# Layer 1 of a fused linear-attention and two-layer kernel: three blocks take turns at 6, 5 and 5 features instead of two blocks at 11 and 5, and fp64 weight tiles land in their own places

## The chip, the cores and the metric

One core of one Trainium2 chip. The metric is device time in microseconds from the first to the last instruction of one launch; lower is better. The kernel before takes 913.98 us, the median of 3 runs (913.88 to 915.51).

## The reference, cut to what matters

```python
B, H, S, D = 4, 8, 768, 48; d_model, d_ff = 384, 2048; n_tokens = B * S = 3072
for t in range(S):                       # linear attention with a decaying state
    state = alpha[:, :, t, :, None] * state + einsum('bhd,bhe->bhde', k[:, :, t], v[:, :, t])
    y[:, :, t] = einsum('bhd,bhde->bhe', q[:, :, t], state)
x = y as (3072, 384)
h = x @ w_in1                            # layer 1: a rational function of h, and |h| in its denominator
P = a0 + a1*h + a2*h**2 + a3*h**3;  Q = 1 + |b0|*|h| + |b1|*h**2
x = (P / (Q + 1e-6)) @ w_out1
h = x @ w_in2                            # layer 2
out = (h * cos(h)) @ w_out2
```

The four weight matrices arrive as fp64, so every weight is turned into fp32 on the chip.

## The kernel before, in words

**Attention.** The 768 steps are cut into 6 chunks of 128 (`C`), and a chunk of one batch is a unit: 24 units (`NU`). The loop at the end of the program runs n from -3 to 24; each pass issues the loads that are due (`load`, L243: `kq` 512 KB, `a` 258 KB, `v` 192 KB a unit), stores of finished outputs (`y_store`, L435), fetches of weights (`w_fetch`, L156), and then `attention(n)` (L457), which spreads the work of five units over the engines. On POOL (GpSimd) a pass has two `affine_select` on the score tiles (L346), a product for q (`scale_q`, L323) and one for k (`scale_k`, L318). On PE (TensorE) a pass has scores (L332), the part of the output from the state (L399) and from the scores (L409), the update (L366) and transposes (L354).

**Weights.** A weight tile is 128 x 384 fp64, 384 KB. `w_fetch` loads it raw; `tick` (L186) turns it into fp32 in three steps: two ACT (ScalarE) copies (L72, L73), then one DVE (VectorE) operation (L77), then a second (L78). `w_hi` (L206) rounds it on ACT (L215), and `w_lo` (L218) puts the rest beside it on POOL (L225). PE multiplies hi and lo parts apart, three passes for a product. Layer 1 has 32 tiles, 16 of `w_in` (one a feature, 128 columns of d_ff) and 16 of `w_out`. `SOME` (L28) says in which passes of attention a tile is fetched: 15 in all. Raw tiles land in a free `x` buffer called `spare`, in two `raw` buffers, and later in the place of `a`. `w_order` sorts the tiles by the slot that needs them. `late` gives the outputs of attention's units 8 to 23 the places of the 16 weight tiles that are needed last, until `y_store` has put them into DRAM in slots 1 to 16 of layer 1.

**Layer 1.** A slot n is one call of `layers(n)` (L1228): the first product of one feature of one block of 512 tokens (`gemm1`, L562, 9 matmuls), the steps of `rational` (L615) for the features of the last four slots, the second product of the feature of slot n - 5 (`gemm2`, L578, 9 matmuls into three accumulators), and at the end one or two steps of `tick`. Six blocks of 16 features make 96 slots. Slot 0 comes with attention's pass 20, so the last passes share the engines with slots 0 to 4. `where(n)` (L524) says which block and feature a slot has: block 0 takes features 0 to 10, block 1 the same, then both take features 11 to 15, and blocks 2 to 5 follow with 16 each. So the weights are needed over 32 slots and not over 16. Because block 1 comes between, block 0's accumulators go out to SBUF at the end of a turn: `acc_out` (L586) copies them on ACT (L593), three copies a turn, and adds them on DVE (L597) to the accumulators of the last turn. `x_load` (L674), `x_hi` (L702) and `x_lo` (L706) bring a block's input and split it, one third a slot, in three slots ahead of its first turn.

In a slot DVE has L628, L631, L632, L633 and L640, and ACT L608, L636, L637, L645 and L646; POOL has L613, L638 and L639. The bank that `gemm1(n)` writes is one of four, and comes free when DVE has done L633 of slot n - 1.

**Layer 2** follows with its own order; its 32 weight tiles are fetched and turned during the rest of layer 1 (`w_fetch(3 * NF ...)` from slot 32 on, one step a slot).

All work is issued in the order of the program on each engine, and every DMA goes through SP's queue.

```python
        if n < 2 * H1:
            return 0, *divmod(n, H1)
        if n < 2 * NF:
            blk, f = divmod(n - 2 * H1, NF - H1)
            return 0, blk, H1 + f
...
        if n < 2 * NF:
            if n > 1:
                tick(2 if n > 4 else 1, 1)
        elif n < N1 - NF:
            if not split:
                tick(1, 1)
```

Of the kernel before, what the change touches and what calls it, by code (L numbers as in the profile page):

```python
# [42 lines left out]
def attn_then_two_moe(ctx, tc, kqT, aT, vP, w1i, w1o, ma, mb, w2i, w2o, out):  # L43
# [109 lines left out]
    def in_spare(i):  # L153
        return i < sum(SOME[:-1]) and i % 6 < 4

    def w_fetch(upto):  # L156
# [9 lines left out]
        if in_spare(i):  # L166
            flat = spare[:, 2 * DM * (i % 6):2 * DM * (i % 6 + 1)]
        elif more and i % 4 < 2:
            if not raw_a:
                raw_a.append(const.tile([128, 3 * HP * (C + 1)], I32, tag="a", name="raw_a"))  # L170
            flat = raw_a[0][:, 2 * DM * (i % 2):2 * DM * (i % 2 + 1)]
        else:
            flat = raw_p.tile([128, 2 * DM], I32, tag="raw", name="raw")
# [379 lines left out]
    def gemm1(n):  # L553
# [3 lines left out]
        x = xt[m, blk]  # L557
        i = 0
        for kk in range(NK):
            ks = slice(kk * 128, (kk + 1) * 128)  # L560
            for w, xx in PASSES:
                nc.tensor.matmul(h, ws[0][f][:, w, ks], x[:, xx, kk, :], start=i == 0, stop=i == 8)  # L562
# [964 lines left out]
```

## Time and profile before

| what | us |
|---|---|
| median of 3 runs | 913.98 (913.88 to 915.51) |
| the profiled execution's own time | 913.8 |
| its span, first to last instruction | 912.1 |
| PE busy | 892.4 (98%) |
| POOL busy | 702.9 (77%) |
| ACT busy | 697.1 (76%) |
| DVE busy | 693.9 (76%) |

The granted TensorE clock is 0.996 of full speed over the span. A view by windows gives the busy time of each engine in each stretch; a timeline gives one row for each instruction (or run of equal ones), with start and duration, and in brackets the idle time of the engine before it and what ended that.

### The profile page before, as it was taken

What the parts mean: (1) busy time and instruction counts of PE and PEld (TensorE: products, weight loads), DVE (VectorE), ACT (ScalarE), POOL (GpSimd) and SP (SyncE); (2) the same over time, 40 slices, a digit from 0 to 9 for tenths busy, and PEclk for the clock granted to TensorE, in tenths of its full rate; (3) what the DMA queues carried; (4) which work ended last, traced back from release to release, by engine and by line L of the source; (5) the groups of instructions that cost most, each with busy time, mean ns of one, the idle gap of its engine ahead of it and who ended that gap; (6) DMA issues with size and microseconds to landing.
All of it is one profiled execution on the core that took longest, in us unless ns stands there. A gap on an engine that the chain in (4) does not pass through costs nothing.

```text
span 912.1 us, 16494 instructions
## 1 busy us (share of the span) xinstructions
PE 892.4 (98%) x5732; PEld 741.2 (81%) x5732; DVE 693.9 (76%) x1247; ACT 697.1 (76%) x1302; POOL 702.9 (77%) x699
## 2 busy tenths in 40 slices
PE   7999999999999999999999999999999999999997
PEld 7788777887788888888888888878888888888885
DVE  7989799998999989989979767666366554555552
ACT  5999898989889788888788778656577666666653
POOL 6899998999889888889879668669787475655332
PEclk9999999999999999999999999999999999999999
DMA  8999545211233141232165276630243433533432
GB/s 281 357 366 370 191 124 196 82 63 36 104 107 94 57 142 45 87 107 94 53 205 185 95 238 239 202 110 27 74 134 109 161 113 96 167 102 105 139 105 90
DMA packets 67307, 128.87 MB, mean 141 GB/s; under 512 B 6928, under 2 KB 30224, under 8 KB 67216
## 3 DMA queue, kind: packets, MB, share of 16 engines
q1 hardware_dynamic: 67216, 127.74, 43.1%
q8 instruction: 47, 0.77, 0.4%
q14 instruction: 44, 0.36, 0.1%
HBM read 95.21 MB, written 32.51 MB: 140 GB/s over the span
## 4 chain that ended last, share of the span: by engine, by line
PE 72%; DVE 8%; ACT 7%; POOL 6%; DMA 4%; issue 2%; SPq 0%; DVEq 0%; ACTq 0%
PE acc L578 22%; PE b L562 18%; PE acc L1054 15%; PE b L1019 6%; PE r L1019 5%; PE r L562 4%; POOL kq L323 2%; POOL kq L318 2%; DMA kq<-kqT 2%; DVE g L628 1%; DVE z L631 1%; ACT b L645 1%; DVE g L640 1%; DMA a<-aT 1%; PE b L1198 1%
## 5 line engine op out<-in xcount | busy, mean ns | idle before, releaser
L578 PE MATMUL acc<-hi,w 128*128 128x512 f32 x738 | 252.5, 396 | 0.0
L562 PE MATMUL b<-x,w 128*128 128x512 f32 x927 | 233.8, 397 | 1.3 <-DVE g L633 1.1
L613 POOL TENSOR_TENSOR lo<-g,hi 128x512 fp32r<-128x512 f32 x128 | 170.2, 1330 | 66.2 <-ACT hi L608 59.4
L562 PEld LDWEIGHTS b<-x,w 128*128 128x128 f32 x927 | 173.4, 188 | 45.4 <-DVE g L633 4.1
L578 PEld LDWEIGHTS acc<-hi,w 128*128 128x128 f32 x738 | 138.7, 188 | 33.9
L1111 POOL TENSOR_TENSOR lo<-g,hi 128x512 fp32r<-128x512 f32 x64 | 83.0, 1297 | 103.6 <-ACT hi L1110 91.6
L578 PE MATMUL acc<-lo,w 128*128 128x512 f32 x369 | 145.7, 395 | 0.0
L639 POOL TENSOR_TENSOR z<-z,ah 128x512 f32<-128x512 f32 x96 | 124.7, 1299 | 8.0
L1054 PE MATMUL acc<-hi,w_out 128*128 128x512 f32 x384 | 130.3, 395 | 0.0
L608 ACT ACTIVATE hi<-g 128x512 fp32r<-128x512 f32 x128 | 80.4, 628 | 47.8 <-PE acc L578 32.6
L578 PEld LDWEIGHTS acc<-lo,w 128*128 128x128 f32 x369 | 69.4, 188 | 16.5
L638 POOL TENSOR_SCALAR z<-ah,cq 128x512 f32<-128x512 f32 x96 | 74.4, 775 | 5.5 <-ACT ah L636 5.4
L1054 PE MATMUL acc<-lo,w_out 128*128 128x512 f32 x192 | 76.4, 398 | 0.4 <-POOL lo L1111 0.2
L1054 PEld LDWEIGHTS acc<-hi,w_out 128*128 128x128 f32 x384 | 68.7, 188 | 9.9
L640 DVE TENSOR_TENSOR g<-g,b 128x512 f32<-128x512 f32 x72 | 49.1, 682 | 16.2 <-ACT g L637 16.0
L636 ACT ACTIVATE ah<-b 128x512 f32<-128x512 f32 x72 | 42.8, 594 | 19.9 <-PE b L562 19.6
L562 PE MATMUL r<-x,w 128*128 128x512 f32 x225 | 56.8, 397 | 1.0 <-DVE g L633 1.0
L1096 DVE SCALAR_TENSOR_TENSOR ah<-z,b 128x512 f32<-128x512 int32 x44 | 30.2, 685 | 35.9 <-ACT z L1092 35.9
L637 ACT ACTIVATE g<-b,cq 128x512 f32<-128x512 f32 x72 | 56.1, 779 | 0.0
L633 DVE SCALAR_TENSOR_TENSOR g<-g,cq,b 128x512 f32<-128x512 f32 x72 | 53.9, 748 | 2.5
L628 DVE SCALAR_TENSOR_TENSOR g<-g,cq,b 128x512 f32<-128x512 f32 x72 | 53.4, 742 | 0.5
L645 ACT ACTIVATE b<-z,lnb 128x512 f32<-128x512 f32 x72 | 50.1, 696 | 4.7 <-DVE g L628 4.0
(202 smaller groups left out, 2028.7 us busy)
## 6 DMA issues: line engine op xcount, KB each, us to landing
w_out<-wd SPq DMA_DIRECT2D x64, 384.0 KB, 3.1
kq<-kqT SPq DMA_DIRECT2D x24, 512.0 KB, 6.6
w<-wd SPq DMA_DIRECT2D x16, 384.0 KB, 3.1
wd<-w SPq DMA_DIRECT2D x16, 384.0 KB, 2.6
a<-aT SPq DMA_DIRECT2D x23, 258.0 KB, 5.8
raw<-w2o SPq DMA_DIRECT2D x14, 384.0 KB, 3.9
v<-vP SPq DMA_DIRECT2D x24, 192.0 KB, 6.6
x<-x1d SPq DMA_DIRECT2D x18, 256.0 KB, 4.2
```

The lines of the kernel that those rows point to most:

```text
L562: nc.tensor.matmul(h, ws[0][f][:, w, ks], x[:, xx, kk, :], start=i == 0, stop=i == 8)
L578: nc.tensor.matmul(acc[k], ws[1][f][:, w, ks], d[g], start=first and i == 0, stop=last and i == 2)
L608: nc.scalar.activation(out=t["hi"], in_=t["g"], func=AF.Copy)
L613: eng.tensor_tensor(out=t["lo"], in0=t["g"], in1=t["hi"].bitcast(F32), op=ALU.subtract)
L628: nc.vector.scalar_tensor_tensor(g, g, cq[:, 3:4], two["h"], ALU.add, ALU.mult)
L638: nc.gpsimd.tensor_scalar(zz, ah, cq[:, 1:2], cq[:, 0:1], ALU.mult, ALU.add)
L639: nc.gpsimd.tensor_tensor(out=zz, in0=zz, in1=ah, op=ALU.mult)
L640: nc.vector.tensor_tensor(out=g, in0=g, in1=h, op=ALU.mult)
L645: nc.scalar.activation(out=r, in_=two["z"], func=AF.Ln, scale=LN_S, bias=lnb)
L1019: nc.tensor.matmul(tile[:, half], w[p], x[q], start=start and i == 0, stop=True, skip_group_check=True)
L1054: nc.tensor.matmul(acc[k], item["w"][:, w, ks], item[g], start=first, stop=last)
L1111: nc.gpsimd.tensor_tensor(out=p["lo"], in0=p["g"], in1=p["hi"].bitcast(F32), op=ALU.subtract)
```

## The change

Three blocks take turns in layer 1: block 0 has features 0 to 5, then block 1, then block 2; then each in turn 6 to 10, then each 11 to 15. Layer 1's weights are needed over 48 slots. Attention fetches 10 tiles and not 15, the first in pass 6, and 7 are turned when slot 0 begins. Steps of `tick` go on at two a slot up to slot 43 for layer 1's tiles and then, again at two, for layer 2's `w_in` (before: one a slot), and one in a slot that splits x or adds. A turn's accumulators are copied out on ACT after the first turn alone; after the second DVE adds them into the same place, after the third DVE adds them for the output. Raw tiles of layer 1 land in the weight's own place, so `spare` is gone; a tile whose place still holds an output is fetched in the slot after that output's store was issued. Block 1's x is loaded in slot 0 and split in slots 3 to 5 (before: 3, and 5 to 7); block 2's is loaded in slot 6 into the places of `a` and `v` and split in slots 9 to 11 (before: loaded in slot 26, split in 28 to 30).

```diff
-H1 = 11
+H1 = 6
+OFFS = 0, 6, 11, NF
 NO = 0
-SOME = [0, 0] + 5 * [1, 1, 0] + [1, 1, 1, 2]
+TURN = 3
+S2 = 44
+SOME = [0] * 6 + 5 * [1, 0, 1]
...
+    def group(f):
+        return sum(f >= i for i in OFFS[1:-1])
+
     w_order = sorted(
         [(0, s, i) for i in range(NF) for s in range(2)],
-        key=lambda w: (w[2] + 5 * w[1] + (H1 if w[2] >= H1 else 0), w[1])
+        key=lambda w: (w[2] + 5 * w[1] + (TURN - 1) * OFFS[group(w[2])], w[1])
     ) + [(1, s, i) for s in range(2) for i in range(NF)]
...
-    spare = x_p.tile([128, 2, NK, TB], F32R, tag="x", name="spare").rearrange("p a b c -> p (a b c)").bitcast(I32)
...
-        if i >= upto or len(steps) > 5 or sum(not in_spare(j) for j in range(i - len(steps), i + 1)) > most:
+        if i >= upto or len(steps) > 5:
             return
         w = w_order[i]
+        if w[0] == 0:
+            if 2 * NF - NU + KEEP <= i > slot[0] - LEAD - 2 + 2 * NF - NU + KEEP:
+                return
+            flat = wp.tile([128, 2 * DM], I32, tag=f"w{w[1]}_{w[2]}", name="raw")
...
-        if n < 2 * H1:
-            return 0, *divmod(n, H1)
-        if n < 2 * NF:
-            blk, f = divmod(n - 2 * H1, NF - H1)
-            return 0, blk, H1 + f
+        if n < TURN * NF:
+            g = group(n // TURN)
+            blk, f = divmod(n - TURN * OFFS[g], OFFS[g + 1] - OFFS[g])
+            return 0, blk, OFFS[g] + f
         return m, *divmod(r, NF)
 
     def in_parts(m, blk):
-        return m == 0 and blk < 2
+        return m == 0 and blk < TURN
...
-                nc.scalar.activation(out=part(blk, k), in_=acc[k], func=AF.Copy)
+                if group(f) == 0:
+                    nc.scalar.activation(out=part(blk, k), in_=acc[k], func=AF.Copy)
+                else:
+                    added[0] = slot[0]
+                    nc.vector.tensor_tensor(out=part(blk, k), in0=part(blk, k), in1=acc[k], op=ALU.add)
                 continue
...
+        if (m, blk) == (0, 2):
+            if kk == 0:
+                for tag, words in (("a", 3 * HP * (C + 1)), ("v", 4 * VW)):
+                    t = const.tile([128, words], F32R, tag=tag, name=f"x_{tag}")
+                    x2.append(t[:, :NK * TB].rearrange("p (a t) -> p a t", a=NK))
...
-        if n < NF:
-            nxt, at, load = (0, 1), n - 5, n == 3
-        elif n < 2 * NF:
-            at, load = n - 2 * NF + 4, n == 2 * NF - 6
+        if n < 2 * NF:
+            nxt, at, load = ((0, 1), n - H1 + 3, n == 0) if n < H1 else ((0, 2), n - 9, n == H1)
...
-            w_fetch(2 * NF if n < 2 * NF else 3 * NF + NO if n < N1 - NF else 4 * NF)
+            w_fetch(2 * NF if n < S2 else 3 * NF + NO if n < N1 - NF else 4 * NF)
...
-        if n < 2 * NF:
+        if n < S2:
             if n > 1:
-                tick(2 if n > 4 else 1, 1)
+                tick(2 if n > 4 and not split and added[0] < slot[0] else 1, 1)
         elif n < N1 - NF:
             if not split:
-                tick(1, 1)
+                tick(2 if added[0] < slot[0] else 1, 1)
```

How the instructions move. Line numbers of the changed kernel are its own: L333, L328, L356 and L235 are L323, L318, L346 and L225 of before; L649 to L661 are L628 to L640; L80 and L81 are L77 and L78; L75, L76 and L225 on ACT are L72, L73 and L215; L610 is the copy-out L593, L728 the x split's ACT half L702, L613 the new add.

POOL, attention's passes 6 and 7, before (`w0_0` and `w0_1` are the first two weight tiles):

```order
L323 TENSOR_TENSOR kq_100<-kq_100,p_506 128x512
L318 TENSOR_TENSOR kq_100<-kq_100,z_658 128x512
L225 TENSOR_TENSOR w0_0_110<-st_105,w0_0_110 128x384
L346 AFFINE_SELECT hi_672<-hi_672 128x512
L346 AFFINE_SELECT lo_674<-lo_674 128x512
L323 TENSOR_TENSOR kq_100<-kq_100,p_580 128x512
L318 TENSOR_TENSOR kq_100<-kq_100,z_741 128x512
L225 TENSOR_TENSOR w0_1_111<-st_105,w0_1_111 128x384
```

and the same passes now:

```order
L333 TENSOR_TENSOR kq_100<-kq_100,p_481 128x512
L328 TENSOR_TENSOR kq_100<-kq_100,z_628 128x512
L356 AFFINE_SELECT hi_638<-hi_638 128x512
L356 AFFINE_SELECT lo_640<-lo_640 128x512
L333 TENSOR_TENSOR kq_100<-kq_100,p_551 128x512
L328 TENSOR_TENSOR kq_100<-kq_100,z_705 128x512
```

The weight rows have left; POOL's first one now stands in pass 10. Ahead of slot 0 there are 7 of them, where there were 10: those of passes 6, 7 and 9 are gone, those of passes 10, 12, 13, 15, 16, 18 and 19 stay.

DVE, from the last row of slot 27 to that of slot 28, before:

```order
L640 TENSOR_TENSOR g_3190<-g_3190,b2_3121 128x512
L77 SCALAR_TENSOR_TENSOR r1_3213<-st_105,r1_3213 128x384
L628 SCALAR_TENSOR_TENSOR g_3190<-g_3190,cq_67,b2_3121 128x512
L631 SCALAR_TENSOR_TENSOR z_3141<-z_3141,b1_3080 128x512
L632 SCALAR_TENSOR_TENSOR b1_3080<-z_3141,b1_3080 128x512
L633 SCALAR_TENSOR_TENSOR g_3140<-g_3140,cq_67,b1_3080 128x512
L640 TENSOR_TENSOR g_3237<-g_3237,r0_3168 128x512
```

and now:

```order
L661 TENSOR_TENSOR g_3174<-g_3174,b2_3109 128x512
L81 SCALAR_TENSOR_TENSOR st_102<-raw_2836,r1_3150 128x384
L613 TENSOR_TENSOR kq_100<-kq_100,acc0_3005 128x512
L613 TENSOR_TENSOR kq_100<-kq_100,acc1_3009 128x512
L613 TENSOR_TENSOR kq_100<-kq_100,acc2_3013 128x512
L649 SCALAR_TENSOR_TENSOR g_3174<-g_3174,cq_67,b2_3109 128x512
L652 SCALAR_TENSOR_TENSOR z_3129<-z_3129,b1_3065 128x512
L653 SCALAR_TENSOR_TENSOR b1_3065<-z_3129,b1_3065 128x512
L654 SCALAR_TENSOR_TENSOR g_3128<-g_3128,cq_67,b1_3065 128x512
L661 TENSOR_TENSOR g_3218<-g_3218,r0_3155 128x512
```

Three adds stand ahead of the slot's own five rows. Such triples stand in slots 28, 33, 38, 43, 48 and 53; before they stood in slots 32 and 37 alone. A step of `tick` (L77/L80 or L78/L81) stands right ahead of all of them but that of slot 43; two stand ahead of that of slot 53.

ACT, from slot 10's L645 to slot 11's L637, before:

```order
L645 ACTIVATE b0_2327<-z_2391,lnb_96 128x512
L646 ACTIVATE b0_2327<-b0_2327 128x512
L72 ACTIVATE st_105<-raw_a_2320 128x384
L73 ACTIVATE r1_2457<-raw_a_2320 128x384
L608 ACTIVATE hi_2470<-g_2346 128x512
L636 ACTIVATE ah_2478<-b2_2418 128x512
L637 ACTIVATE g_2479<-b2_2418,cq_67 128x512
```

and now:

```order
L666 ACTIVATE b0_2296<-z_2363,lnb_96 128x512
L667 ACTIVATE b0_2296<-b0_2296 128x512
L225 ACTIVATE w0_8_2414<-st_102 128x384
L728 ACTIVATE x_a_2241<-x_v_2242 128x512
L75 ACTIVATE st_102<-raw_2239 128x384
L76 ACTIVATE r1_2430<-raw_2239 128x384
L610 ACTIVATE kq_100<-acc0_2184 128x512
L629 ACTIVATE hi_2445<-g_2315 128x512
L610 ACTIVATE kq_100<-acc1_2188 128x512
L610 ACTIVATE kq_100<-acc2_2192 128x512
L657 ACTIVATE ah_2455<-b2_2386 128x512
L658 ACTIVATE g_2456<-b2_2386,cq_67 128x512
```

The stretch now holds a rounding, an x split and three copies-out besides. Copies-out stand in slots 11, 17 and 23; before they stood in slots 16 and 27.

## Rows read from the trace of the kernel before

**Rows 1.** View by windows: stretch, then each engine's busy us (instructions), PEclk, DMA share, GB/s.

```profile
21.70:53.90 32.20, 29.24 (x607) 25.27 (x605) 28.89 (x76) 28.71 (x59) 28.64 (x32) 1.00 1.01 368
53.90:97.40 43.50, 41.50 (x843) 36.71 (x842) 39.73 (x105) 40.92 (x83) 43.22 (x48) 1.00 1.03 357
...
150.20:209.80 59.60, 59.60 (x257) 48.05 (x257) 56.73 (x91) 54.92 (x104) 56.72 (x53) 1.00 0.27 82
...
244.60:300.00 55.40, 55.40 (x237) 44.66 (x238) 53.74 (x83) 47.88 (x84) 50.08 (x45) 1.00 0.33 106
```

**Rows 2.** Timeline of POOL in attention: start us, us, line, operation (passes 14, 15 and 16; 15 has a weight row).

```profile
71.72 1.27 POOL L323 TENSOR_TENSOR kq<-kq,p 128x512 f32<-128x512 f32 x1
...
75.36 1.28 POOL L323 TENSOR_TENSOR kq<-kq,p 128x512 f32<-128x512 f32 x1
...
79.95 1.29 POOL L323 TENSOR_TENSOR kq<-kq,p 128x512 f32<-128x512 f32 x1
```

**Rows 3.** View of POOL's waits, 20 to 104 us: us in total, times, longest us.

```profile
POOL kq L323 <- DMA kq<-kqT: 3.7, 4, 2.1
```

**Rows 4.** DMA view of 21.7 to 53.9 us: issues with KB each, median us to landing.

```profile
spare<-w1i SPq DMA_DIRECT2D x3, 384.0 KB, 7.1
```

**Rows 5.** Timeline of SP's queue, passes 3 and 4.

```profile
22.99 0.54 SPq L257 DMA_DIRECT2D kq<-kqT  x1
23.58 0.90 SPq L174 DMA_DIRECT2D spare<-w1i  x1
...
29.83 0.33 SPq L257 DMA_DIRECT2D kq<-kqT  x1
```

**Rows 6.** Timeline of PE, first products of slots 0, 7, 27, 28, 29, 32, 33 and 34.

```profile
99.08 2.37 PE L562 MATMUL b<-x,w 128*128 128x512 f32 x9
...
132.46 2.36 PE L562 MATMUL r<-x,w 128*128 128x512 f32 x9 [0.96 <-DVE g L633]
...
217.41 2.27 PE L562 MATMUL r<-x,w 128*128 128x512 f32 x9
221.61 2.27 PE L562 MATMUL b<-x,w 128*128 128x512 f32 x9
226.63 2.37 PE L562 MATMUL b<-x,w 128*128 128x512 f32 x9 [0.67 <-DVE g L633]
...
239.77 2.27 PE L562 MATMUL b<-x,w 128*128 128x512 f32 x9
244.60 2.37 PE L562 MATMUL b<-x,w 128*128 128x512 f32 x9 [0.46 <-DVE g L633]
248.90 1.33 PE L562 MATMUL b<-x,w 128*128 128x512 f32 x5
```

**Rows 7.** Timeline of DVE, slots 26 to 28, and the adds of slots 32 and 37.

```profile
216.41 0.68 DVE L640 TENSOR_TENSOR g<-g,b 128x512 f32<-128x512 f32 x1
217.01 0.56 DVE L77 SCALAR_TENSOR_TENSOR r<-st,r 128x384 int32<-128x384 int32 x1
...
218.07 0.74 DVE L628 SCALAR_TENSOR_TENSOR g<-g,cq,b 128x512 f32<-128x512 f32 x1
...
220.84 0.68 DVE L640 TENSOR_TENSOR g<-g,b 128x512 f32<-128x512 f32 x1
223.25 0.56 DVE L77 SCALAR_TENSOR_TENSOR r<-st,r 128x384 int32<-128x384 int32 x1 [1.73 <-ACT r L73]
...
226.50 0.68 DVE L640 TENSOR_TENSOR g<-g,r 128x512 f32<-128x512 f32 x1
...
239.90 1.87 DVE L597 TENSOR_TENSOR o<-kq,acc 128x512 f32<-128x512 f32 x3
...
260.30 2.09 DVE L597 TENSOR_TENSOR o<-kq,acc 128x512 f32<-128x512 f32 x3 [0.51 <-PE acc L578]
```

**Rows 8.** Timeline of ACT, the copies-out of slot 27.

```profile
217.52 0.59 ACT L593 ACTIVATE kq<-acc 128x512 f32<-128x512 f32 x1
...
218.51 1.09 ACT L593 ACTIVATE kq<-acc 128x512 f32<-128x512 f32 x2
```

More of the change, by code (lines that the diff above doesn't have):

```diff
@@ L114, in attn_then_two_moe @@
     kq_t = [kq_all[:, i] for i in range(5)]
-    v_t = [const.tile([128, H * D + 64 - D], F32, tag=f"v{i}", name=f"v{i}") for i in range(4)]
+    VW = H * D + 64 - D
+    v_all = const.tile([128, 4, VW], F32, tag="v", name="v")
+    v_t = [v_all[:, i] for i in range(4)]
     st_all = const.tile([128, 4, DM], F32, tag="st", name="st")
@@ L159, in w_fetch @@
         fetched[1] = upto
-        more = LEAD + 5 <= slot[0] < LEAD + N1
-        most = 4 if more else 2
-        if i >= upto or len(steps) > 5 or sum(not in_spare(j) for j in range(i - len(steps), i + 1)) > most:
+        if i >= upto or len(steps) > 5:
             return
         w = w_order[i]
-        fetched[0] += 1
[L166 to L173, printed above, removed]
+        if w[0] == 0:
[3 more added lines that the diff above has]
+        else:
+            more = LEAD + TURN * NF + 2 <= slot[0] < LEAD + N1
+            if len(steps) + 1 > (4 if more else 2):
+                return
+            if more and i % 4 < 2:
+                if not raw_a:
+                    raw_a.append(const.tile([128, 3 * HP * (C + 1)], I32, tag="a", name="raw_a"))
+                flat = raw_a[0][:, 2 * DM * (i % 2):2 * DM * (i % 2 + 1)]
+            else:
+                flat = raw_p.tile([128, 2 * DM], I32, tag="raw", name="raw")
+        fetched[0] += 1
         nc.sync.dma_start(out=flat, in_=(w1i, w1o, w2i, w2o)[2 * w[0] + w[1]][w[2]].bitcast(I32))
@@ L452, in convert @@
                 turn[:] = [2, 0, 0, 3, 0]
-        assert n != LEAD + 2 or place or not steps[0][1]
+        assert n != LEAD + 2 or place or not (steps and steps[0][1])
         tick(turn[place], 2 if n < LEAD else 1)
@@ L556, in gemm1 @@
         h = h_bank(n)
-        x = xt[m, blk]
+        x = [x_part(m, blk, i) for i in range(2)]
         i = 0
@@ L561, in gemm1 @@
             for w, xx in PASSES:
[L562 removed]
+                nc.tensor.matmul(h, ws[0][f][:, w, ks], x[xx][:, kk], start=i == 0, stop=i == 8)
                 i += 1
@@ L569, in gemm2 @@
         assert m or (0, 1, f) in ready
-        first = f == 0 or in_parts(m, blk) and f == H1
-        last = f == NF - 1 or in_parts(m, blk) and f == H1 - 1
+        first = f == 0 or in_parts(m, blk) and f in OFFS
+        last = f == NF - 1 or in_parts(m, blk) and f + 1 in OFFS
         for k in range(NK):
@@ L596, in acc_out @@
             if in_parts(m, blk):
+                added[0] = slot[0]
                 nc.vector.tensor_tensor(out=o, in0=part(blk, k), in1=acc[k], op=ALU.add)
@@ L674, in x_load @@
     def x_load(m, blk, kk):
-        if kk == 0 and (m, blk) not in xt:
+        if (m, blk) == (0, 2):
[3 more added lines that the diff above has]
+                    x2.append(t[:, :NK * TB].rearrange("p (a t) -> p a t", a=NK))
+        elif kk == 0 and (m, blk) not in xt:
             xt[m, blk] = x_p.tile([128, 2, NK, TB], F32R, tag="x", name="x")
-        x = xt[m, blk][:, 1, kk, :].bitcast(F32)
+        x = x_part(m, blk, 1)[:, kk].bitcast(F32)
         ks = slice(kk * 128, (kk + 1) * 128)
@@ L700, in x_hi @@
     def x_hi(m, blk, kk):
-        x = xt[m, blk]
-        nc.scalar.activation(out=x[:, 0, kk, :], in_=x[:, 1, kk, :].bitcast(F32), func=AF.Copy)
+        hi, lo = (x_part(m, blk, i)[:, kk] for i in range(2))
+        nc.scalar.activation(out=hi, in_=lo.bitcast(F32), func=AF.Copy)
     def x_lo(m, blk, kk, eng=None):
-        hi, lo = (xt[m, blk][:, i, kk, :] for i in range(2))
+        hi, lo = (x_part(m, blk, i)[:, kk] for i in range(2))
         (eng or nc.vector).tensor_tensor(out=lo, in0=lo.bitcast(F32), in1=hi.bitcast(F32), op=ALU.subtract)
@@ L875, in w_first @@
         elif t == 3:
-            v = [const.tile([128, 3 * 128], F32R, tag=f"v{i}", name=f"w_v{i}") for i in range(4)]
+            v_w = const.tile([128, 4, VW], F32R, tag="v", name="w_v")
+            v = [v_w[:, i, :3 * 128] for i in range(4)]
             hi, lo = v[:2], v[2:]
@@ L1294, in attn_then_two_moe @@
         nc.gpsimd.memset(lnb, LN_S * ONE_EPS)
-        for t in v_t:
-            nc.gpsimd.memset(t[:, H * D:], 0.0)
+        nc.gpsimd.memset(v_all[:, :, H * D:], 0.0)
         nc.gpsimd.memset(ident, 1.0)
```

17 lines of the change are left out of this document (10 added, 7 removed).

## The prediction

> **What bounds the kernel now.** I read the view by windows first, then the timelines of POOL, SP, PE and DVE where they touch the change. Attention is full everywhere. In passes 3 to 9 (21.7 to 53.9 us) the DMA engines' share is 1.01 at 368 GB/s, and PE is busy for 29.24 of 32.20 us, POOL for 28.64 [rows 1]. In passes 10 to 19 the share is 1.03 and POOL is busy for 43.22 of 43.50 us. So POOL sets the pace late in attention, and early in it POOL and DMA take turns: POOL waits four times for a `kq` load, 3.7 us in all [rows 3]. A pass without a weight row takes POOL 75.36 - 71.72 = 3.64 us, one with a weight row 79.95 - 75.36 = 4.59 us [rows 2]; a weight costs POOL 0.95 us a pass.
>
> In layer 1 PE is the bound, but barely. From 150.2 to 209.8 us it is busy for the whole window, DVE for 56.73 of 59.60 us, POOL for 56.72, ACT for 54.92 [rows 1]. PE's slot is 221.61 - 217.41 = 4.20 us [rows 6]. A DVE slot with both weight steps takes 220.84 - 216.41 = 4.43 us, of which L77 and L78 take 218.07 - 217.01 = 1.06 [rows 7]; so its own five rows take 3.37 us and one step about 0.47 to 0.5. Two tiles in three slots make DVE 3 x 3.37 + 2 x 1.06 = 12.2 us against PE's 12.6. DVE's lead is what to watch: `gemm1` of the next slot may start 0.13 us after the row of L640 does (226.63 against 226.50 for slot 28, where L640 follows L633), so at slot 27 the usable lead is 221.61 - 220.84 - 0.13 = 0.64 us [rows 6, 7]. Where the lead is spent, PE waits for L633: 0.96 us at slot 7, 0.67 at slot 29, 0.46 at slot 33 [rows 6].
>
> **The change part by part**, against the profiled execution's 913.8 us (0.2 below the median of 913.98).
>
> 1. *Attention.* Three weight rows leave POOL (passes 6, 7, 9): 3 x 0.95 = 2.9 us. Ahead of pass 10 three tiles fewer are loaded: 3 x 0.393 MB = 1.18 MB, at 368 GB/s [rows 1] 3.2 us of DMA. If POOL alone counted, the gain would be 2.9 + 3.7 = 6.6 us. If the `kq` waits stay because SP hands the loads out no sooner, it would be near nothing: the `kq` loads of passes 3 and 4 are issued 29.83 - 22.99 = 6.84 us apart, and the weight between them takes 0.90 us of the queue [rows 5]. PE keeps all its work, 29.24 of 32.20 us, which leaves 2.96. DMA's 3.2 and PE's 2.96 lie nearest to each other, so I take **-3.0**, with 0 and -6.6 as ends. A load's removal has a price in the notes too: the Trainium skill, "DMA: Bandwidth & Descriptors", section Bandwidth, measures 425 GB/s for one core's 16 MB load, by which the estimate for 1.18 MB is 2.8 us and the forecast would be 0.2 us later. This stretch moved 368 GB/s at a share of 1.01, so the trace decides. From pass 10 to 19 the seven weight rows stay where they were, so nothing more is gained. In slot 0 one of two weight rows goes: 0 to -0.95 us; I take 0, since scores, outputs and first products then stand back to back on PE.
> 2. *Slots 3 to 13.* Block 1's splits move two slots up, beside attention's last passes: at most the 0.96 us of slot 7 is saved [rows 6]. Block 2's splits come into slots 9 to 11, with ACT's first copies-out among them. Three copies take ACT 0.59 + 1.09 = 1.7 us [rows 8], and DVE's half of a split waits for ACT's. I put 0.6 of it on PE: **-0.4**, ends -1.0 and +1.7.
> 3. *Copies-out in slots 17 and 23.* On both sides of the copies ACT and DVE have the rows of slot 27 before: a rounding, a copy, L608, two copies, then the next tile's L72 and L73, for which DVE's L77 waits. There L77 waited 1.73 us and slot 29 began 226.63 - 221.61 = 5.02 us after slot 28, 0.82 too late [rows 6, 7]. Twice that is **+1.6**; ends 0 and 2 x 1.73 = 3.5.
> 4. *DVE's triples of adds*, six where there were two. A triple takes 1.87 us [rows 7], 1.8 of it ahead of the next row. A slot with a triple and one weight step takes 3.37 + 0.47 + 1.8 = 5.64 us, 1.44 more than PE's. Two slots with one step give back 0.36 each, one with two takes 0.22. So slot 28 comes with a lead of 0.5 and loses 0.9; slots 33 and 38 come with 0.86 and lose 0.6 each; slot 43 has four slots without steps ahead of it and loses nothing, as at slot 37 before, where DVE even waited 0.51 us for PE [rows 7]; slot 48 loses 0.6, slot 53 (both steps, 6.23 us, lead 1.3) 0.7. Sum **+3.4**. The ends are 0, if every triple rides like that of slot 37, and 5 x 1.8 = 9.0, if all but that of slot 43 are passed on whole.
> 5. *Stalls that go.* Block 2's splits leave slots 28 to 30 and no triple stands in slot 32. From slot 28 to slot 34 PE took 248.90 - 221.61 = 27.29 us, for 6 x 4.20 = 25.2 [rows 6]: **-2.1**.
> 6. *At nothing.* Layer 2's `w_in` steps at two a slot from slot 44: DVE's 12.2 us for three slots lie under PE's 12.6, as from 150.2 to 209.8 us, where PE lost nothing [rows 1]. From 244.6 to 300 us, with one step a slot, DVE was busy for 53.74 of 55.40 us, so the cover is thin; if it goes, rival B's refill goes too. Raw tiles that wait for an output's store: `w_fetch` runs up to six tiles ahead, about nine slots, and a tile lands in 7.1 us [rows 4]; what queues behind it on SP are the next store and block 2's x, three slots ahead of its split. Layer 2 and the tail only shift.
>
> Sum: -3.0 - 0.4 + 1.6 + 3.4 - 2.1 = -0.5. From the profiled 913.8 that is 913.3; from the runs' median of 913.98, which a timing will be set beside, **913.5 us**. A measurement of this kernel can tell about 0.2% (1.8 us) from no change, so the forecast is no change.
>
> **The rivals.** *A, the debts are not passed on* (faster). PE loses only where DVE's lead is gone; if the lead at slot 28 is 1.4 us or more, parts 3 and 4 cost nothing and the time is 913.98 - 3.0 - 0.4 - 2.1 = 908.5; with half of them paid, 911.0. For it: slot 37's triple cost nothing and DVE waited for PE. Against it: the lead of 0.64 us at slot 27 after 20 slots at the same load.
>
> *B, the triples are passed on whole* (slower). In slots 28, 33, 38, 48 and 53 DVE comes without a lead, because the refill of 0.36 a slot is eaten by waits for ACT such as the 1.73 us of slot 27. Then part 4 costs 9.0 and not 3.4: 919.1; half way there, 916.3. It decides between a refill of 0 and 0.5 us from one triple to the next. For it: DVE, POOL and ACT are within 8% of full at 150.2 to 209.8 us. Against it: slot 33 before lost less than its triple.
>
> *C, attention is no shorter* (slower). SP hands out `kq` after stores that wait for the engines, so the 3.7 us of waits grow by what POOL gains; part 1 is 0 and the time 916.5. For it: 6.84 us between two `kq` loads, of which the weight's issue is 0.90. Against it: a DMA share of 1.01 with the tiles in it.
>
> **How the numbers follow.** Forecast 0.43, A 0.33, B 0.13, C 0.11. Faster by over 0.2% is A, 0.33; within 0.2% the forecast, 0.43; slower B and C, 0.24. The likeliest case's own range is 912.2 to 915.8, the bound of what can be told apart. For 8 in 10 the range takes A from its half way to near its full price and B and C up to just past C: 909.5 to 917.0; about 0.1 is left out on each side, for A's full price with a better part 1, and for B beyond its half way.
>
> **What would show it.** In the changed profile slot 0's first product should start about 3 us before 99.08 us [rows 6]; POOL's waits for `kq` should be near 3 us in passes 3 to 9 (near nothing for a gain of 6.6, above 6 for C). PE should show waits for L654 (L633 before) at slots 18 or 19, 24 or 25, 29, 34, 39, 49 and 54, of 0.4 to 0.9 us each, none at slot 44, and none past slot 60. L80 should wait for L76 (L77 for L73) in slots 17 and 23. If those waits are missing, A holds; if they are 1.5 us and more at the triples, B. A stall of PE for a weight tile or an x load, in any slot, would make this prediction wrong in its plan, not only in a size.

## The result, and the profile after

| | before | after |
|---|---|---|
| median, 4 runs each | 914.58 us (913.88 to 915.51) | 923.77 us (923.07 to 924.72) |
| ratio of the runs | | 1.0101, 95% interval 1.0083 to 1.0118 |
| profiled execution, span | 913.8, 912.1 | 923.5, 921.8 |
| PE busy | 892.4 (98%) | 894.4 (97%) |
| first product of slot 0 | 99.08 [rows 6] | 97.76 |
| first product of slot 118 | 601.70 | 611.37 |

The change costs 9.2 us, 1%. From slot 118 to the end both kernels take the same: 921.8 - 611.37 = 310.4 and 912.1 - 601.70 = 310.4. So the loss lies ahead of slot 118: attention is 1.3 us shorter, and the layers are 11.0 us longer. I take it apart with the starts of the first products. PE of after, timeline: start us, us, line, tiles, count, and in brackets PE's idle time and what ended it; slots 0, 13, 18, 19, 25, 29, 34, 39, 54, 78, 101, 102 and 103.

```profile
97.76 2.36 PE L577 MATMUL b<-x,w 128*128 128x512 f32 x9
...
158.57 0.50 PE L577 MATMUL b<-x_a,w 128*128 128x512 f32 x1 [0.40 <-DVE g L654]
...
179.64 2.26 PE L577 MATMUL b<-x,w 128*128 128x512 f32 x9
184.96 2.37 PE L577 MATMUL r<-x,w 128*128 128x512 f32 x9 [0.95 <-DVE g L654]
...
211.32 2.37 PE L577 MATMUL b<-x,w 128*128 128x512 f32 x9 [0.91 <-DVE g L654]
...
229.41 0.50 PE L577 MATMUL b<-x_a,w 128*128 128x512 f32 x1 [1.02 <-DVE g L654]
...
251.32 2.37 PE L577 MATMUL b<-x,w 128*128 128x512 f32 x9 [0.66 <-DVE g L654]
...
273.24 2.37 PE L577 MATMUL r<-x,w 128*128 128x512 f32 x9 [0.65 <-DVE g L654]
...
337.11 2.37 PE L577 MATMUL b<-x,w 128*128 128x512 f32 x9 [0.63 <-DVE g L654]
...
439.22 2.37 PE L577 MATMUL b<-x,w 128*128 128x512 f32 x9 [0.34 <-DVE g L654]
...
535.93 2.26 PE L577 MATMUL b<-x,w 128*128 128x512 f32 x9
542.66 3.77 PE L577 MATMUL b<-x,w 128*128 128x512 f32 x9 [2.37 <-DVE g L681]
548.37 2.26 PE L577 MATMUL b<-x,w 128*128 128x512 f32 x9
```

Slot 18 to 19 is 184.96 - 179.64 = 5.32 us where a slot takes 4.20, and 0.10 more goes in the slot behind. The last rows are the largest loss: 548.37 - 535.93 = 12.44 us for two slots, 4.0 over 8.4. What stands before them on SP, DVE and POOL of after (timelines, same columns):

```profile
535.74 1.27 SPq L859 DMA_DIRECT2D w_f<-wf  x3
```

```profile
535.12 0.55 DVE L81 SCALAR_TENSOR_TENSOR st<-raw_a,r 128x384 int32<-128x384 int32 x1
538.71 3.30 DVE L759 TENSOR_TENSOR w_f<-w_f 128x128 f32<-128x128 f32 x4 [3.04 <-DMA w_f<-wf]
541.93 0.68 DVE L681 TENSOR_TENSOR g<-ah,b 128x512 f32<-128x512 f32 x1
```

```profile
538.23 0.47 POOL L759 TENSOR_TENSOR w_f<-w_f 128x128 f32<-128x128 f32 x1 [4.24 <-DMA w_f<-wf]
538.65 1.29 POOL L634 TENSOR_TENSOR lo<-g,hi 128x512 fp32r<-128x512 f32 x1
539.90 1.04 POOL L235 TENSOR_TENSOR w<-st,w 128x384 fp32r<-128x384 f32 x1
540.90 0.50 POOL L759 TENSOR_TENSOR w_f<-w_f,w_f 128x128 f32<-128x128 f32 x1
541.36 0.50 POOL L759 TENSOR_TENSOR w_f<-w_f 128x128 f32<-128x128 f32 x1
```

Layer 2's planner loads rows of weights (`w_stage`, L859) into the place of `a`. The load is issued 0.07 us after L81 has turned the last raw tile that lay there (`raw_a`). The adds on those rows (L759) stand ahead of L681 in the program's order, so L681 and PE wait for the load.

And POOL, whose own add had waited 4.24 us, then runs the rows it is late with beside DVE's four adds, which take 3.30 us where they took 0.89 in before and in e1. PE's wait begins at 542.66 - 2.37 = 540.29 us, and PE starts 0.73 us after L681 does. With adds of 0.89 us L681 would have started near 539.5 and PE near 540.3: an estimate from these rows, by which the late load and the slow adds make the wait together. No run has one without the other; e1 below takes both away.

In the kernel before, the last tile in `raw_a` was turned at 524.70 us, the load issued at 525.31, and the adds ran at 530.45 without a wait (DVE, SP and DVE of before):

```profile
524.70 0.55 DVE L78 SCALAR_TENSOR_TENSOR st<-raw_a,r 128x384 int32<-128x384 int32 x1
...
525.31 1.27 SPq L833 DMA_DIRECT2D w_f<-wf  x3
...
530.45 0.89 DVE L733 TENSOR_TENSOR w_f<-w_f 128x128 f32<-128x128 f32 x4
```

Behind the wait PE also ran at the lower clock; view by windows of after (stretch, busy us of PE, PEld, DVE, ACT, POOL, granted clock, DMA share, GB/s):

```profile
540.00:542.00 2.00, 0.29 (x2) 0.00 (x0) 1.99 (x5) 0.00 (x0) 1.86 (x3) 1.00 1.04 402
542.00:544.00 2.00, 1.34 (x3) 1.15 (x4) 1.97 (x5) 1.30 (x3) 0.59 (x1) 0.59 1.04 404
544.00:546.00 2.00, 2.00 (x6) 1.52 (x6) 1.97 (x5) 1.73 (x4) 1.77 (x2) 0.56 0.54 124
546.00:548.00 2.00, 2.00 (x10) 1.59 (x9) 1.60 (x4) 0.00 (x0) 0.47 (x2) 1.00 0.82 324
```

Of the 4.0 us, 2.4 are the wait. The other 1.6 are mostly the clock's (0.56 to 0.59 of 2.4 GHz, so mostly the 1.2 GHz level): in e3 a wait of 2.29 us without a fall cost slots 102 and 103 together 2.56, which leaves about 1.4 for the fall.

Attention was 4.7 us ahead at pass 10 and lost 3.5 of it by pass 18. POOL's L323 and L333, passes 10 and 18, before and then after:

```profile
53.92 1.28 POOL L323 TENSOR_TENSOR kq<-kq,p 128x512 f32<-128x512 f32 x1
...
88.20 1.29 POOL L323 TENSOR_TENSOR kq<-kq,p 128x512 f32<-128x512 f32 x1
```

```profile
49.19 1.28 POOL L333 TENSOR_TENSOR kq<-kq,p 128x512 f32<-128x512 f32 x1
...
86.98 1.28 POOL L333 TENSOR_TENSOR kq<-kq,p 128x512 f32<-128x512 f32 x1
```

In between PE stopped in the middle of eight products of the same two tiles (16 rows, 13 of them ahead of the stop), for a reason that no semaphore shows ("issue"), and the clock fell behind it (timeline, then windows as above):

```profile
64.17 0.56 PE L376 MATMUL u<-v,g 128*64 128x48 f32 x13
67.40 0.32 PE L376 MATMUL u<-v,g 128*64 128x48 f32 x3 [2.67 <-issue]
```

```profile
66.00:68.00 2.00, 0.60 (x6) 0.54 (x6) 1.05 (x5) 0.00 (x0) 2.00 (x4) 0.98 1.07 301
68.00:70.00 2.00, 2.00 (x31) 1.67 (x33) 0.12 (x1) 1.40 (x3) 1.82 (x2) 0.50 1.07 287
70.00:72.00 2.00, 2.00 (x32) 1.83 (x26) 1.81 (x4) 1.47 (x4) 0.74 (x2) 0.67 1.05 301
```

The DMA view of 64 to 66 us (queue: packets, MB, share of 16 engines' time) has one 16 KB piece on the queue for instructions, beside `kq` and the rest on engines that are full; that the stop is for this piece is not shown:

```profile
q1 hardware_dynamic: 405, 0.73, 100.2%
q8 instruction: 1, 0.02, 3.4%
```

### The profile page after: what moved, and what is told of

Same layout as the page of the kernel before. It is cut to its first block, busy times and chain, and to the rows that moved or that the text cites. A ratio compares the mean times of both kernels' runs of the same rounds, so it can differ in the third digit from the quotient of the medians.

```text
span 921.8 us, 16517 instructions
## 1 busy us (share of the span) xinstructions
PE 894.4 (97%) x5732; PEld 740.0 (80%) x5732; DVE 705.2 (77%) x1259; ACT 697.8 (76%) x1302; POOL 703.4 (76%) x696
## 4 chain that ended last, share of the span: by engine, by line
PE 60%; DVE 20%; ACT 11%; issue 4%; POOL 3%; DMA 1%; DVEq 0%; POOLq 0%; ACTq 0%; SPq 0%
PE acc L1081 15%; PE acc L593 12%; PE b L577 11%; PE b L1046 6%; PE r L1046 5%; DVE g L649 3%; DVE g L661 3%; DVE z L652 3%; DVE b L653 2%; DVE g L654 2%; PE sc L342 2%; PE r L577 2%; PE b L419 2%; ACT b L666 2%; PE b L409 2%
## 5 line engine op out<-in xcount | busy, mean ns | idle before, releaser
L593 PE MATMUL acc<-hi,w 128*128 128x512 f32 x738 | 251.9, 395 | 0.0
L577 PE MATMUL b<-x,w 128*128 128x512 f32 x819 | 208.6, 399 | 5.8 <-DVE g L654 3.3
L577 PEld LDWEIGHTS b<-x,w 128*128 128x128 f32 x819 | 153.8, 189 | 46.7 <-DVE g L654 6.9
L593 PEld LDWEIGHTS acc<-hi,w 128*128 128x128 f32 x738 | 138.6, 188 | 33.5
L593 PE MATMUL acc<-lo,w 128*128 128x512 f32 x369 | 145.8, 395 | 0.0
L660 POOL TENSOR_TENSOR z<-z,ah 128x512 f32<-128x512 f32 x96 | 125.3, 1305 | 8.0
L593 PEld LDWEIGHTS acc<-lo,w 128*128 128x128 f32 x369 | 69.3, 188 | 16.7
L654 DVE SCALAR_TENSOR_TENSOR g<-g,cq,b 128x512 f32<-128x512 f32 x72 | 53.9, 748 | 2.5
L661 DVE TENSOR_TENSOR g<-g,b 128x512 f32<-128x512 f32 x72 | 49.0, 680 | 7.5 <-ACT g L658 7.3
L649 DVE SCALAR_TENSOR_TENSOR g<-g,cq,b 128x512 f32<-128x512 f32 x72 | 53.4, 742 | 0.4
L681 DVE TENSOR_TENSOR g<-ah,b 128x512 f32<-128x512 f32 x31 | 21.3, 687 | 40.5 <-ACT ah L679 40.5
L653 DVE SCALAR_TENSOR_TENSOR b<-z,b 128x512 f32<-128x512 f32 x72 | 50.1, 696 | 2.5
```

Of the source, the lines that this page charges most:

```text
L577: nc.tensor.matmul(h, ws[0][f][:, w, ks], x[xx][:, kk], start=i == 0, stop=i == 8)
L593: nc.tensor.matmul(acc[k], ws[1][f][:, w, ks], d[g], start=first and i == 0, stop=last and i == 2)
L649: nc.vector.scalar_tensor_tensor(g, g, cq[:, 3:4], two["h"], ALU.add, ALU.mult)
L654: nc.vector.scalar_tensor_tensor(g, g, cq[:, 2:3], r, ALU.add, ALU.mult)
L660: nc.gpsimd.tensor_tensor(out=zz, in0=zz, in1=ah, op=ALU.mult)
L661: nc.vector.tensor_tensor(out=g, in0=g, in1=h, op=ALU.mult)
```

## The experiments

"Lateness" below is the start of a first product, counted from slot 0, against the same count in the kernel before. At slot 118 it is 10.99 us in after; a second profile of before (e11) differs from the first by 0.05. A run's median is over several executions, its first product and lateness are from one profiled execution. "Before" medians beside the runs were 914.5 to 915.0 us.

**e1: w_f's place free in time.**

```diff
-            if more and i % 4 < 2:
+            if more and i % 4 < 2 and slot[0] < LEAD + N1 - 6:
```

> The changed kernel, except that a layer-2 tile may land in the place of `a` only when it is fetched before slot 90; so tile 53 lands in a `raw` buffer and the last tile in the place of `a` is turned one and a half slots earlier. Theory (the 4.0 us of slots 102 and 103 come from the rows of w_f, whose load waits until that tile is turned, so that the planner's adds wait in DVE's and POOL's queues in front of L681): PE's wait for L681 at slot 102 is gone, the granted clock stays full after it, and the time is 923.8 - 4.0 = 919.8 us. Rival (DVE and POOL are late there for their own work, a tile's steps and the adds in one slot): the wait stays, 923.8.

Measured 919.69 us (ratio to before 1.0062, 1.0043 to 1.0081). The wait for L681 is gone, the clock is 1.00, and the same first products come 4.20 us apart:

```profile
532.62 2.26 PE L577 MATMUL b<-x,w 128*128 128x512 f32 x9
536.82 2.26 PE L577 MATMUL b<-x,w 128*128 128x512 f32 x9
541.02 2.26 PE L577 MATMUL b<-x,w 128*128 128x512 f32 x9
```

The theory holds: where the last raw tile lands costs 4.0 us. Slots 71 to 79 lost 0.2 us here and 1.3 in after, though the program ahead of slot 90 is the same; part 6 below has the rows in which the two executions part.

**e2: no adds of the second turn.**

```diff
-                    nc.vector.tensor_tensor(out=part(blk, k), in0=part(blk, k), in1=acc[k], op=ALU.add)
```

> The changed kernel without the second turn's nine adds (features 6 to 10 of blocks 0 to 2 are left out of the output). Theory (each triple of adds on DVE is passed on to PE in part): the stalls at slots 29, 34 and 39 (1.2, 0.8 and 0.8 us over 4.20) go, those at slots 13, 19, 25 and 54 stay: 923.8 - 2.8 = 921.0 us. Rival (the steps of tick and the splits have eaten DVE's lead by then and the stalls come without the adds too): no change, 923.8.

Measured 919.67 us (1.0045, 1.0030 to 1.0059). Slots 29, 34 and 39 take 4.19 to 4.20 us each, lateness at slot 118 is 7.95, 3.0 less; slots 13, 19, 25 and 54 stay at 5.31, 5.28, 5.27 and 4.98. The theory holds. The median fell by 4.1; the 1.1 beyond is not in the layers, and the profile's attention was 0.9 us shorter (first product at 96.85), as it may be in any execution.

**e3: no copies-out of the first turn.**

```diff
-                    nc.scalar.activation(out=part(blk, k), in_=acc[k], func=AF.Copy)
+                    pass
```

> The changed kernel without the first turn's nine copies-out on ACT; the second turn's adds are kept at their place and length, but take the part times zero (features 0 to 5 of blocks 0 to 2 are left out of the output). Theory (three copies of ACT in one slot make a tile's steps late, on which DVE and then PE wait): the stalls at slots 13, 19 and 25 (1.1 us each over 4.20) go, 923.8 - 3.3 = 920.5 us. Rival (slot 13 comes from block 2's splits and the lead is short anyway): slot 13 stays and slots 29 and 34 stay as they are, 923.8 - 2.2 = 921.6 us or above.

Measured 919.62 us (1.0043, 1.0028 to 1.0058). Slots 19 and 25 fall to 4.20 us, slot 13 stays at 5.29: theory for two of three, rival for slot 13. Slot 29, which should have stayed, fell from 5.38 to 4.90. PE waited 2.29 us for L681 here too, but the granted clock stayed at 1.00 behind it, so the fall does not follow every such wait.

**e4: one step from slot 62.**

```diff
-                tick(2 if added[0] < slot[0] else 1, 1)
+                tick(2 if n < 62 and added[0] < slot[0] else 1, 1)
```

> The changed kernel with one step of tick a slot from slot 62 on, as in the kernel before, and two only up to slot 61. From slot 62 on the weight tiles are then fetched and turned in the same slots as in the kernel before, so the last tile in the place of `a` is turned by slot 99. Theory: the stalls at slots 71 to 73 and 78 (1.2 us together) go and so does the 4.0 us of slots 102 and 103: 923.8 - 5.2 = 918.6 us. Rival (those stalls come from the three copies of a block's end on ACT, not from the second step): 919.8 us.

Measured 919.36 us (1.0047, 1.0033 to 1.0062). Lateness stays at 5.57 us from slot 55 to slot 118, 5.4 less than in after: without the second step slots 71 to 79 lose nothing, and with before's schedule the place of `a` is free in time.

**e5: attention without eight of its loads.**

```diff
+            if slot[0] <= LEAD:
+                if w[1] not in shared:
+                    shared[w[1]] = raw_p.tile([128, 2 * DM], I32, tag="raw", name="raw")
...
+                raw64[w] = shared[w[1]].rearrange("p (a b) -> p a b", b=2)
```

> The kernel with one step from slot 62 on, but every tile that attention fetches is turned from one of two raw tiles, a w_in and a w_out, that are loaded once (so the weights of features 0 to 5 and a few more are wrong copies); every step stays on its engine. Eight loads of 0.393 MB fall away, 3.1 MB, at the 366 GB/s of passes 3 to 9 8.6 us of DMA time. Theory (full DMA engines hold attention up, in late `kq` tiles and in PE's own code, whose 16 KB pieces arrive late): POOL's waits for `kq` and PE's waits for `issue` between 22 and 95 us go, and the first product of slot 0 comes at POOL's own pace: pass 3 at 21.7 us, 17 passes of 3.64 and 7 weight rows of 0.95 give 90.2, and 1.5 to the first product 91.7, where five profiles of the same attention had 95.5 to 99.7 (mean 97.5); time 919.4 - 5.8 = 913.6 us. Rival (the engines bound attention, the waits are of their order): first product at 95.5 to 99.7, 919.4 us.

Measured 916.68 us (1.0010, 0.9998 to 1.0023), first product at 96.64 us. Neither side: 2.7 us were gained of the 5.8, and the runs lie closer together (915.5 to 917.6, e4's 916.8 to 922.6). POOL still waited 2.8 us for `kq` before pass 10, of which 2.3 ended at 35.04 us, ahead of the first weight load (issued at 36.79), and PE 1.5 us for "issue" at 54.78, at a DMA share of 0.97 from 22 to 54 us and 0.91 from 54 to 76. So the loads are a part of what holds attention, not all of it, and PE's stops for "issue" are not shown to come from them.

**e6: no steps beside copies-out and adds.**

```diff
+REST = 17, 23, 28, 33, 48, 53
...
-                tick(2 if n > 4 and not split and added[0] < slot[0] else 1, 1)
+                tick(0 if n in REST else 2 if n > 4 and not split and added[0] < slot[0] else 1, 1)
```

> The kernel with one step from slot 62 on (here from slot 64), and no step of tick at all in slots 17, 23, 28, 33, 48 and 53, those in which accumulators are copied out or added. Theory (a copy-out or a triple costs PE what is left of it after DVE's and ACT's lead, so the steps beside it decide): the lateness at slots 19 and 25 falls from 1.1 us each to 0.2, at 29, 34 and 54 from 1.2, 0.8 and 0.8 to 0.7, 0.3 and 0.3, those at 13 and 39 stay: 919.4 - 3.3 = 916.1 us. Rival (the rows of a copy-out or a triple are passed on whole whatever stands beside them): no change, 919.4 us.

Measured 916.90 us (1.0017, 0.9999 to 1.0036). Slots 19 and 25 take 4.20 us, 34, 39 and 54 4.7 (39 should have stayed), but 29 keeps 5.52, and 49 and 62 lose 0.4 and 0.6 anew: lateness 3.41 against e4's 5.57. The steps beside a copy-out decide what it costs PE; slot 29 did not follow.

**e8: eight fetches in attention.**

```diff
-SOME = [0] * 6 + 5 * [1, 0, 1]
+SOME = [0] * 9 + 4 * [1, 0, 1]
```

> The kernel with one step from slot 62 on, with 8 tiles fetched in attention and not 10 (the first in pass 9) and 5 turned when slot 0 begins; the steps go on three slots longer, up to slot 40. Theory (a tile in attention costs POOL 0.95 us and the DMA engines 1.07 us, which are both full there): first product 2 us earlier, at a mean of 95.5, 917.4 us. Rival 1 (attention's waits eat the gain, as they ate most of the gain of five tiles): 919.4 us. Rival 2 (weights late: PE waits for a tile of the last turn, whose slack is one slot): 921 us or above.

Measured 917.38 us (1.0032, 1.0017 to 1.0046), first product at 95.65 us. Both numbers are the theory's, but neither decides alone: e4's interval (1.0033 to 1.0062) overlaps this one, and profiles with ten tiles have had 95.48 too. Slots 39 to 44 are as in e4, so no weight was late; slot 49 lost 0.4 us that it does not lose in e4 (lateness 6.02 against 5.57).

**e9 and e10: block 0's x spread over attention** (e6 and e8 with this edit).

```diff
-            if n >= 8 and x_pieces:
+            if n in (8, 10, 11, 13, 14, 16, 17, 18):
```

> The kernel of e6_rest, with the eight loads of block 0's x in passes 8, 10, 11, 13, 14, 16, 17 and 18 and not in passes 8 to 15. Theory (attention is held up by full DMA engines where x, weights and `kq` come together, 328 to 338 GB/s at a share of 1.05 from 54 to 76 us): POOL and PE lose less in passes 10 to 15 than they gain later, first product 1.5 us earlier than e6's 97.8, 916.9 - 1.5 = 915.4 us. Rival (the order of the loads on the queue changes only when the same bytes are waited for): 916.9 us.

> The kernel of e8_eight_fetches with the same eight loads of x spread as in e9. Theory: first product 1.5 us earlier than e8's 95.65, 917.4 - 1.5 = 915.9 us. Rival: 917.4 us.

Measured 915.25 us (1.0003, 0.9989 to 1.0017) and 916.10 us (1.0014, 1.0000 to 1.0028), ratios 0.0014 and 0.0018 (1.3 and 1.6 us) under e6's and e8's. The intervals overlap, so each gain alone is weak, though both medians moved by what was expected. The first products came at 97.27 and 94.38 us, 0.5 and 1.3 earlier and not 1.5. What is shown is the sum: e10 differs from e4 by the eight fetches and the spread alone, their intervals do not touch (1.0033 to 1.0062 and 1.0000 to 1.0028), and the layers are no shorter (lateness 6.04 and 5.57). So the two edits together gave back about 3 us of attention.

**e11: before, once more.**

> The kernel before, unchanged, for a second profile of its attention. Theory (attention's length differs from execution to execution by some us, by when `kq` and code of PE land): the first product differs from 99.08 us by 0.5 us or more, and the layers behind it keep their length (from slot 0 to slot 117 within 0.2 us). Rival (attention of the kernel before has one length): 99.08 within 0.3 us.

One run, 914.89 us; first product at 99.71 us, layers within 0.05: the theory. That the layers always keep their length it does not show: e13's, with the same code, are 0.5 us longer, and after's differ by 0.4 between its two profiles.

**e12: after, once more.**

> The changed kernel, unchanged. Theory: the layers again lose 10 to 11 us against the kernel before, the first product lies anywhere from 95.5 to 99.7 us; time 923.8 us. Rival (the 4.0 us of slots 102 and 103 was of one execution): 919.8 us.

Measured 924.76 us (1.0109, 1.0081 to 1.0136); first product at 96.89 us, lateness 11.34 at slot 118, and 2.44 us of PE's wait for L681 at slot 102.

**e13: before with x spread** (the edit of e9 alone).

> The kernel before, with the eight loads of block 0's x in passes 8, 10, 11, 13, 14, 16, 17 and 18 and not in passes 8 to 15. Theory (x, weights and `kq` meet on full DMA engines in both kernels): about 1.5 us faster, as e9 against e6 and e10 against e8: 914.6 - 1.5 = 913.1 us. Rival (the kernel before is held by POOL from pass 10 on, which is busy for 22.00 of 22.00 us from 54 to 76 us, so that the loads cost it nothing): no change, 914.6 us.

Measured 914.45 us (0.9996, 0.9985 to 1.0008), first product at 99.24 us: the rival. From 54 to 76 us POOL is busy for 21.72 and 22.00 us in the two profiles of before and for 22.00 here, so the spread had nothing to give there (windows of e13):

```profile
54.00:76.00 22.00, 20.70 (x426) 18.36 (x423) 19.97 (x54) 20.52 (x42) 22.00 (x25) 1.00 1.05 368
```

**e14: block 2's split one slot earlier.**

```diff
-            nxt, at, load = ((0, 1), n - H1 + 3, n == 0) if n < H1 else ((0, 2), n - 9, n == H1)
+            nxt, at, load = ((0, 1), n - H1 + 3, n == 0) if n < H1 else ((0, 2), n - 8, False)
...
+        if n == H1 - 1:
+            for kk in range(NK):
+                x_load(0, 2, kk)
...
-REST = 17, 23, 28, 33, 48, 53
+REST = 11, 17, 23, 48, 53
```

> The kernel of e9, with block 2's x loaded in slot 5 and split in slots 8 to 10 (before: 6, and 9 to 11), no step in slot 11, and in return one step again in slots 28 and 33. Theory (slot 13 comes from the split and the steps that stand beside the copies of slot 11): the 1.1 us at slot 13 falls to 0.2, slots 29 and 34 go back from about 0.7 and 0.4 us of net lateness to 1.1 and 0.8: together 0, 915.3 us. Rival (slot 13 comes from slots 9 and 10, where splits and steps stand too): slot 13 keeps 1.1, the others go back, 916.2 us.

Measured 913.64 us (0.9987, 0.9975 to 1.0000), the fastest, at the edge of what can be told from before, and under both forecasts. Slot 13 falls from 5.32 to 4.31 us, but slots 10 and 11 now take 4.84 and 5.28, and slot 29 4.20, which neither side expected; lateness is 2.52 against e9's 3.22, and the first product came at 95.16 against 97.27, so most of the gain on e9 in the profiles is attention, which this edit leaves alone. The lateness of slot 13 went with the split. Two of its three DVE rows are long, and PE waits 0.47 and 0.81 us for DVE's L655 (after's L654) behind them (timeline of e14, slots 8, 9 and 10):

```profile
137.84 1.78 DVE L733 TENSOR_TENSOR x_v<-x_v,x_a 128x512 fp32r<-128x512 f32 x1
...
142.90 1.53 DVE L733 TENSOR_TENSOR x_v<-x_v,x_a 128x512 fp32r<-128x512 f32 x1
...
148.18 0.68 DVE L733 TENSOR_TENSOR x_v<-x_v,x_a 128x512 fp32r<-128x512 f32 x1
```

## Why the prediction was wrong, by its own steps

The prediction had 913.5 us, no change, and 909.5 to 917.0 as its range; 923.77 lies outside. Lateness against before, in us, profile of after:

| part | forecast | measured | where |
|---|---|---|---|
| 1 attention | -3.0 | -1.3 | slot 0 |
| 2 slots 3 to 13 | -0.4 | +1.4 | slots 0 to 14 |
| 3 copies-out | +1.6 | +2.3 | slots 19, 25 |
| 4 triples | +3.4 | +4.0 | 29: 1.3; 34, 39, 54: 0.9 each |
| 5 stalls that go | -2.1 | -2.1 | slots 28 to 34 |
| 6 "at nothing": two steps a slot | 0 | +1.3 | slots 72 to 79 |
| 6 "layer 2 only shifts" | 0 | +4.0 | slots 102, 103 |
| sum | -0.5 | +9.6 | 9.7 by the spans |

**The step that failed most** is the last sentence of part 6, "Layer 2 and the tail only shift". Layer 2's tiles were turned at another pace, so another tile was the last in the place of `a`, and a load that had been issued 5.1 us ahead of its use (525.31 to 530.45) kept DVE waiting for 3.0 us. The prediction priced the steps of `tick` as engine time and never asked whose place each raw tile holds. e1 shows it: with the place free in time the wait, the slow adds behind it and the clock's fall are gone, and slots 102 and 103 take 4.20 us.

**Part 6, the pace.** The forecast's "under PE's 12.6" counted steady slots: DVE's five rows and two tiles' steps in three slots. In slot 70 three copies of a block's end stand on ACT besides (L622, 400.88 to 402.94 us), and ahead of slot 78 two split rows of 1.5 us on DVE. Without the second step none of seven profiles loses anything in slots 71 to 79 (e4, e5, e8, e10, and e6, e9, e14 from slot 64); with it all five do, 1.3 to 1.4 us in four of them and 0.2 in e1. The executions part at a split row near slot 60 (timelines of POOL and DVE, after and then e1):

```profile
365.82 1.30 POOL L660 TENSOR_TENSOR z<-z,ah 128x512 f32<-128x512 f32 x1
365.85 1.82 DVE L732 TENSOR_TENSOR x<-x 128x512 fp32r<-128x512 f32 x1
```

```profile
363.61 1.86 POOL L660 TENSOR_TENSOR z<-z,ah 128x512 f32<-128x512 f32 x1
363.63 0.68 DVE L732 TENSOR_TENSOR x<-x 128x512 fp32r<-128x512 f32 x1
```

The two rows meet within 0.03 us, and one of them takes longer. In after it is DVE's, as in the other three (1.81 to 1.82 us), and DVE loses 1.1 us of its lead; in e1 it is POOL's. The row is long in e4 too (1.79 us), and nothing is lost there: the full 1.3 us takes the long row and the second step together.

**Part 3** named the right chain (L80 waits for L76: 1.73 us at 207.94 us, as in [rows 7]) and the right slots; one copy-out costs 1.1 us and not 0.8. The row of the wait, DVE of after:

```profile
207.94 0.56 DVE L80 SCALAR_TENSOR_TENSOR r<-st,r 128x384 int32<-128x384 int32 x1 [1.73 <-ACT r L76]
```

e3 and e6 show that the copies and the steps beside them make it together.

**Part 4** was right in kind: without the adds slots 29, 34 and 39 lose nothing (e2). For slot 54 no run takes the adds away; it falls from 4.99 to 4.67 us when the step beside them goes (e6). That the sum came near is in part luck: four triples cost 0.9 to 1.3 us where 0.6 to 0.9 were forecast, and slot 49 lost nothing where 0.6 was. Rival B's full 9.0 did not come, rival A's zero neither.

**Part 2** forecast a gain because block 1's split moved, and up to slot 11 the layers were 0.3 us ahead; slots 12 to 14 then lost 1.65, 1.1 of it at slot 13, where 0.6 was put on PE. Not the copies make it (e3) but block 2's split (e14 moves it). That DVE's half waits for ACT's was named, and it did, for 0.80 us at 154.60. The DVE row itself was not priced; it took 0.68 to 1.78 us in these slots, by what POOL does beside it (e14, and 1.35 us at 149.08 us in after).

**Part 1** was right in kind up to pass 10 (4.7 us ahead in after, 1.7 to 4.9 in the other profiles of this attention, all against 53.92 us; before's second profile has 54.87). What it missed is the second half: "nothing more is gained" should have been "some is given back". Before had POOL as its pace from pass 10 to 18, 34.28 us, where 8 passes of 3.64 and 5 weight rows of 0.95 make 33.9 [rows 2]; after took 37.8, other profiles of it 34.7 to 36.3 but for e3's 39.4. After and e3 are also the two with the longest stops for "issue" there (2.67 and 2.27 us) and the only two of the seven whose granted clock fell there (in e3 to 0.50 in the rows from 70 to 76 us). The seven profiles with this attention have the first product at 95.5 to 99.7 us, mean 97.5, against 99.08 and 99.71 before: 1.9 us gained on average, not 3.0. e4 and e10 show that fewer loads and another order of them, together, give some back; how much of the rest is PE's stops for "issue" stays open.

Of the signs that the prediction named, the waits at slots 19, 25, 29, 34, 39 and 54, none at 44, and L80 behind L76 came. The first product came 1.3 us and not 3 before 99.08, POOL waited 1.7 us and not 3 for `kq` in passes 3 to 9, slot 49 did not wait, and "none past slot 60" failed: there lies the miss. The chance given to slower was 0.24, but its rivals put the loss in the triples and in attention; 5.3 of the 9.6 us lay in part 6.

## What to carry to other kernels

When a change alters the pace at which buffers are used, follow each shared place (a tag, a pool slot) to its next owner, to the end of the program, and compare the time of the last read with the time of the next load: one row of the order would have shown the wait that cost 4 us here. Price each small loss with what stands beside it in its slot: steps, splits and copies cost PE little here until they met. And a third turn costs its own copies-out, adds and splits: here 5.6 us of layers (parts 2 to 5) for some 2 us of attention.

## What was not expected of the hardware

When an operation between SBUF tiles on DVE meets one on POOL, one of the two takes longer. In after a split row (L732) took 0.68 us where it started ahead of POOL's row (144.65, while POOL's L660 took 1.67 us and not 1.30). Where POOL's row was ahead it took 1.35 and 1.82 us (149.08, 365.85) and ended 0.55 us behind POOL's. The four adds of L759 took 0.89 us together in e1 and 3.30 in after, beside POOL's rows of 1.29, 1.04, 0.50 and 0.50 us, and each of them ended 0.15 us behind the POOL row beside it. The Trainium skill, "SBUF — State Buffer", section "SBUF: two separate sides", says that DVE with two SBUF inputs and a GpSimd operation that reads SBUF lock a port pair, that whichever starts first has it for the whole instruction, and that the other blocks. These rows agree with it. In e1's pair at 363.61 and 363.63 us POOL's row was the long one though its start is recorded 0.02 us earlier, so at that distance the trace does not tell which was first.

PE at times stopped for up to 2.7 us in attention with nothing in the profile to release it, and once a 16 KB piece of instructions moved in that time. After it, as after the wait of slot 102, the granted clock was 0.50 to 0.67 in the next two rows of 2 us, though not after a wait of nearly the same length in e3 (2.29 and 2.37 us); where it fell, a wait of 2.4 us cost 4.0.
